# Attention with beacon keys and a gated feed-forward layer on one core: gate and value weights in two column blocks, under a newly searched instruction order

## The chip, the cores and the metric

The kernel runs on one core of a Trainium2 chip. The core has five engines with an instruction queue each: TensorE (PE in the profile, with PEld for its weight loads), VectorE (DVE), ScalarE (ACT), GpSimd (POOL) and SyncE (SP), and sixteen DMA engines that they share. The metric is device time in microseconds (us), the median of several executions.

## The reference

Inputs are q, k and v of shape 8 batches x 8 heads x 576 positions x 64, 16 extra "beacon" keys and values per head, and three weight matrices: gate and value of 512 x 1,536, output of 1,536 x 512. All are float32.

```
k_all = concat(beacon_k, k); v_all = concat(beacon_v, v)
scores = (q @ k_all.T) / 8, causal: the beacon keys are seen by every row
a = softmax(scores);  x = a @ v_all, heads side by side -> 4608 x 512
out = (relu(x @ w_gate) * (x @ w_val)) @ w_out      -> 4608 x 512, float32
```

## The kernel before

**Attention.** Each batch's q and k are loaded by SP's queue into staging tiles, rounded to bfloat16 (POOL or DVE), transposed on TensorE (L553, L626) and copied from PSUM (L493 on ACT, L495 on DVE). Scores (L824, in 64 x 64 parts of the array; L874 for the last 16 rows of a batch) go to PSUM. DVE adds the mask and takes the row minimum of the negated scores (L772), ACT takes the exponential and its sum (L779), DVE the reciprocal (L785), POOL normalises (L790). The weights are transposed, for batch 0 on TensorE (L900), later by DMA (pTb from pb, pTa from pa), and multiplied with v (L920, for the last rows L943) into the transposed activations xT.

**Feed-forward layer.** Ten spans of positions (240, 336, seven of 512, 448) each go through 12 blocks nf of 128 hidden columns: four gate matmuls (L981), relu on ACT (L992), four value matmuls (L986), the product on DVE (L997). Output products (L1012) follow per 128 positions in three parts of four nf, are copied out and stored.

**Weights.** They stay in SBUF as wg_r, wv_r and wo_r (bfloat16). The function `weight` (L505 to L512) issues one DMA on POOL's queue that reads float32 and writes bfloat16, for all four row blocks of 128 and w columns from n0:

```
x = add("POOL", W_ISSUE, lambda t: nc.gpsimd.dma_start(
    d[:, ko:ko + kos, n0:n0 + w], s[:, ko:ko + kos, n0:n0 + w]), (), (), work, 0.1, move=W_MOVE * kos * w / 512,
    after=W0 + W_STEP * len(weight_in) / KM)
for i in range(kos):
    for c in range(n0, n0 + w, 512):
        weight_in[kind, ko + i, c] = x
```

The loop at L1034 calls it for gate and value of each entry of W_COLS, then three times for the output weights (four blocks of 128 rows each). Below, v0 or g512 mean the transfer of value columns from 0 or gate columns from 512; wo0, wo4 and wo8 the three of the output weights. Blocks nf=0 to 3 use columns 0 to 511, nf=4 to 7 columns 512 to 1,023, nf=8 to 11 columns 1,024 to 1,535.

**The order.** Nothing is scheduled at run time. Work is entered in a plan as tasks with engines, costs and dependences; a search outside this file has put them into one list, and `replay` (L1067) issues the tasks as the string ORDER lists them: an entry is a task's number, a letter for the engine where there is a choice (a ACT, v DVE, g POOL) and the numbers of the buffers that it takes. f4:7 stands for four fill matmuls on ident (L1064) into PSUM bank 7, which do no work of the kernel; they stand in the first 32 us. Each engine works its own part of the list in order; semaphores hold an instruction until its inputs are there. So the order of one engine's queue is fixed, and an instruction that waits holds up all behind it on that engine.

POOL's order of transfers is v0, g0, v512, g512, wo0, v1024, g1024, then much later wo4 and wo8. HELD (L45) ties three loads of batch 1 to weights while an order is searched: at L563 a one-element memset of the staging tile on POOL stands ahead of such a load, and the load on SP's queue comes after the memset.

On TensorE, gate nf=0 of the first span is the 43rd task; gate nf=4, the first to use columns from 512, comes after the value product of batch 0's first head pair that uses L920 on pTb and the last 64 x 64 scores of batch 0's second group. After it come the scores of batch 0's last rows (L874), another value product and gate nf=5.

Of the kernel before, what the change touches and what calls it, by code (L numbers as in the profile page):

```python
# [54 lines left out]
W_COLS = [(0, 512), (512, 512), (1024, 512)]  # L55
# [22 lines left out]
10 1 22:0 2 26:1 34:3 0 4 30:2 23v:0.0 8 38:4 24:0 9 5 f4:7 42:5 27g:1.0 7 25v 48:7 28:1 46:6 35v:0 31v:2 36:3 29v 32:2 50:0 f3:7 37v 33a 54:1 f2:7  # L78
39v:1 410:4.5.0.0 58:2 11 431:6.0 6 40:1 411 43g:2 12 412 41a 423 44:2 413 45a 49g:0 422 3 436 414 448:3.1.0.0 62:7 415 421 f12:7 432 47g 426 68:5 450
416 459 70:6 449 425 460 51g:0 451 469:2.4 424 66:4 f1:7 417 437 461 14 52:5 427 433 55v:1 470 53a 418 56:6 434 f8:7 474 428 463 419 57v 471 429 462  # L80
420 59v:2 486:5.6.0.1 475 430 472 63v:0 454 473 438 487 64:2 453 435 60:7 464 69v 439 491 452 440:4 61a 72:0 476 495:3.1 13 73 441v:0 492 f3:7 455 465
496 488 444:0 467 f2:7 16 65v 504:4.5 497 77:1 489 500 442:2 445a:0 458 f3:7 505 457 f1:7 501 466 513:6.0 493 456 509 446:3 506 477 f1:7 f3:7 502 498
468 514 447a 443a 15 478:3 510 71v 482:4 518 522:1.2 515 19 511 524 479a:0 523:5.6 67g 516 519 483v:0 480:3 512 528 484:4 481a 18 525 548:7.3.2.3 485v
529 549 90:5 494 557:1.2 91 1734:4 553 17 550 1738:0 562 1735:0 566:5.6 507 503 1739:1 f2:7 558 563 1736:4 508 567 1742:7 559 490 1737:0 554 526 520
499 1740:4 571 1743:2 575:1.0 81:3 568 517 1741:1 82 1744:2 576 86:4 572 584:3.4 527 f1:7 580 1746:5 577 521 532:7 569 530 560 586 1747:1 531 536:1
533a:0 1748:5 1745:2 534:6 74:1.1 1749:3 537a 540:2 564 535v 587 78:2.1 95:0 544:5 542:1 541v:1 125:7 538:6 581 570 588 573 585:2.3 551 565 543a 555
539v 1750:0 561 545v 610:6.7.0 590 1751:1 552 546:4 589 578 611 591 1754:0 579 75:5 612 1752:1 1755:0 582 592 547v 76a 1756:3 574 613 1758:2 1757:5
593 594:4 1753:4 1759:0 596:5 556 595v:2 598:1 1762:0 583 614 79:7 597v 1760:4 1763:1 615 599a 602:2 1761:6 80a 606:5 87:1 616:1 604:4 617v:0 83:0
600:3 603v:3 92:2 101:3 84:6 601a 88:7 113:4 605v 607a 93:0 96:0 618:3 105:1 85a 89v 20 109:2 608:2 94a 99:6 97:5 126:1.0 609v 1766:1 98a 1764:4 619a
127:6 620:0.2.0.1 102:2 1765:7 128a 635:3.5 1770:7 1767:2 621 21 643 103:6 628 1768:4 622 1771:0 106:0 104a 1772:1 1769:8 624 1774:7 114:2 1773:9  # L90
1778:4 629 623 123:4 1776:1 1775:1 644 1779:2 1780:6 121:5 110:1 631 1792:4 1777:10 133:1 636 630 650:7.0 137:2 1781:11 1793:0 1787:2 637 129:0 645
646 659 107:6 652 639 111:4 1782:1 632 625 638 647 651 649 108a 112v 115:3 1788 633 653 640 116v 627 654 665:6.5 658 626 674:3.4 634 661 666 1794:7
642 660 670 1783 667 100:1 655 676 671 657 1784 119:6 124 677 700:0.6.2.3 1795:12 1785a:0 122 141:4 1796:5 701 679 117:3 668 656 708 715:7.1 702 678
648 1789 134:1 709 1797:1 704 669 717 145:1 1800:4 176:5 662 1790a:1 1798:3 716 664 723 703 1802:5 663 718 1799:13 641 1801:2 1804:2 724 1786 120 711
675:3.4 672 705 680 1803:14 149:6 1805:0 681 1806:0 726 683 682 1808:2 719 1807:15 673 690:3 1812:5 710 1809:1 712 130:0.0 730:6.0 684 725 1810:7 720
732 686 713 1814:1 738 1813:2 721 731 685 714 1816:5 1811:8 118 131:2 739 734 1818:4 687 1815:1 1817:1 689 745:3.7 733 1819:2 1820:1 688 741 735 746
754:5.6 132a 736 695:1 740 1822:4 750 722 1821:1 1824:0 757 142:0 747 1823:11 1828:1 151:7 707 751 756 755:3.4 138:2 1825:2 727 1832:2 742 748 758 737
763 1826:7 706 1829:0 752 749 1830:0 759 152 1827:4 728 691:1 760 764 693:7 762 692a 1831:5 765 761 780:5.6.1 694v 139:1 781 135:0 753 1833:1 770:2
143:3 766 1836:7 140v 146:1 136a 1834:2 782 729 1837:2 767 147:4 144a 1835:6 1838:0 769 783 148v 744 696:1 698:2 784 1839:10 790:5.6.0.1 785 805:4.7
1840:3 792 160:1 768 791 786:0 799 743 794 1841 177:2.1 775:3 798 697a 813 793 1842 150:0 787v:1 699a 814 801 153:0 788:2 807 800 178:1 1843a:2  # L100
820:0.5 789v 161:2 773:6 179a 828 815 806 771:2 1845:3 795 829 809 156:0 821 808 772v 1846 164:1 816 822 180:7 774v 831 835:2.4 1847 823 840 830 1791
824 817 1850:6 832 172:6 833 841 825 836 170:3 826 844:0.1 1848a:0 819 778:5 810 846 837 834 776:7 1851 811 777a 838 847 796 779a 157:1 154:2 849
845:4.5 184:0 165:0 848 1852 853 839 188:1 192:2 166:3 802 155v 1853a:1 804 162:0 1849 158:7 1855:1 854 812 174:5 850 167v 855 173 168:4 1857:6 163v
852 1856:2 159v 1859:2 827 856 797 857 1858:8 870:7.0.2.3 1860:1 851 885:4.3 1863:5 871 893 872 185:2 860:2 1867:2 886 874 878 842 894 843 1861:6 873
887 1864:2 858 896 1865:7 1862:9 803 1868:0 171 879 1871:5 895 859 888 875 1866:10 818 880 900:6.1 889 169 1869:2 865:1 909 881 175 901 1875:3 908
1872:1 189:0.1 1870:11 911 915:7.4 181:1 902 1873:2 910 890 916 904 892 903 182:1 876 1879:0 183v 193:1 1876:2 210:7 1874:4 917 861:6 863:3 196:2 897
882 862a 912 920 202:6 924:1.2 1880:0 200:1 925:6.7 927 921 1877:5 918 905 926 919 864a 226:0 1881:0 877 1878:13 928 933 914 950:3.4.0 929 868:5 206:5
906 1844 934 866:1 1883:2 930 224:4 867v 935 931 1882:14 1854 186:1 891 1884:1 190:6 187v 1887:0 203:0 191a 951 936 907 194:2 1885:6 932 195a 937 952
197:2 1888:2 940:2 1889:7 1886:15 953 899 869v 1895:1 938 954 1890:0 198:3 207:1 204:0 1891:4 199a 883 205v 884 959:6.5.7.2.0.1 1892:0 939 208:3 218:6
913 961 1893:4 898 209a 220:2 973 211:2 960 1899:0 965 1894:1 955 964 962 1897:3 974 956:0 1896:1 1900:2 963 1901:6 1898:2 967 230:5 941:0 975 943:4  # L110
978 922 976 923 1903:1 977 214:7 944a 1902:3 227:1.0 942a 945:3 1904 966 979 221:1 980 986:5.3.4.6 225 1908:7 987 988 1913:0 215:0 998 991 981 968 201
1909 997 990 989 219 222:4 1910 999 242:1 992 256:6 957:5 1001 212:2 1911a:0 1905 213v 231:2.0 958a 1912 1000 216:5 970 238:2 1002 1906v:2 1914 234:7
993 217v 223 1007:3.4.6.7 946:1 995 250:4 1015 948:2 972 1918:5 949a 971 1016 252:3 985 1009 1915 1017 1907 947v 982 284:5 1008 983 1018 1105:1.2.1
268:0 228:6 1916a:1 1919 1106 1010 1917 1019 235:0 1107 1920 1011 229v 969 246:7 1108 1003 239:1 1923:3 1921v:0 1004 1109 1032:4.0.7.1.2.3 1110 1924:0
1925:2 1034 994 1111:1 996 1931:5 1033 1046 1038 1926:4 251:0 232:6 1927:3 1047 1932:2 264:4 1037 1012 1048 1013 1050 1929:2 1036 1051 1021 236:4 1035
1928:1 1933:5 233v 243:2 1039 1049 1040 1014 272:1 244:7 240:3 1930:5 247:0 237a 1022:0 1935:6 1053 245v 253:1 1112:4 1052 241v 1020 1936:0 1939:0
1934:6 1005 248:2 1113v 257:2 1059:1.5.3.7 249a 254:6 1940:1 1061 1943:4 255a 1070 260:6 1060 1937:2 1041 1944:2 1071 1043 1062 1947:6 1074 984 1054
# [205 lines left out]
def kernel(  # L323
# [774 lines left out]
```

## Time and profile before

| | |
|---|---|
| median of 2 runs | 399.56 us (399.12 to 400.01) |
| the profiled execution | 399.52 us, of which its span, first to last instruction, 397.6 us |
| granted TensorE clock, mean | 0.999 |
| busy: PE, DVE, ACT, POOL | 96%, 69%, 68%, 58% of the span |
| moved by DMA | 68.89 MB, 173 GB/s on average |
| first matmul, first gate matmul (L981), first L1012 | 4.37, 27.55, 51.79 us |

Times in the views are microseconds from the first instruction. A view by stretch gives the busy time of each engine in it; a timeline gives start, length, engine, line, operation, tiles, count, and in brackets how long the engine stood idle before and what released it. Matmul lengths overlap (a matmul's record includes its latency), so start times tell more than lengths. A row "A <- B: total, times, longest" says how long A waited for B. Time to landing runs from a DMA's issue to its semaphore.

### The profile page before, as it was taken

The page shows a single profiled execution, that of the slowest core. Times are in us where ns is not written, and L with a number is a line of the kernel's source. Part 1 is how long each engine was busy: PE and PEld are TensorE (multiplying, and loading weights), DVE is VectorE, ACT ScalarE, POOL GpSimd, SP SyncE. Part 2 cuts the span into 40 slices and gives each one's busy share as a digit, 9 for nine tenths or more (in the row PEclk, how much of TensorE's full clock was granted, in tenths as well). Part 3 has the DMA queues.
Part 4 walks back from the last instruction along what each step waited for, and adds up shares of the span by engine and source line. Part 5 has one row for each costly group of instructions (what it writes and reads, how often), then busy time and mean ns, then how long its engine had stood idle before and what let it go on. Part 6 is the DMA issues. An engine that isn't in the chain of part 4 may idle for free.

```text
span 397.6 us, 10026 instructions
## 1 busy us (share of the span) xinstructions
PE 380.1 (96%) x3384; PEld 199.7 (50%) x3428; DVE 274.2 (69%) x1008; ACT 270.3 (68%) x842; POOL 231.0 (58%) x447
## 2 busy tenths in 40 slices
PE   5789999999999999999999899999999999999996
PEld 3557855655454455454444454445444445444453
DVE  5899799888976888877876778567946832331230
ACT  1899699897877687789777789688746731332322
POOL 3799779959785789268827787663853650000000
PEclk9999999999999999999999999999999999999999
DMA  7999999999999999968997999988897556001102
GB/s 183 218 181 237 193 230 235 195 230 236 215 234 205 313 177 203 181 186 177 202 205 215 197 202 198 209 162 167 169 180 161 101 105 168 28 0 54 54 26 94
DMA packets 184100, 68.89 MB, mean 173 GB/s; under 512 B 158384, under 2 KB 179504, under 8 KB 184048
## 3 DMA queue, kind: packets, MB, share of 16 engines
q1 hardware_dynamic: 179216, 63.46, 74.5%
q0 software_dynamic: 4752, 4.72, 7.3%
q8 instruction: 27, 0.44, 0.5%
q14 instruction: 25, 0.20, 0.1%
q10 hardware_dynamic: 80, 0.07, 0.1%
HBM read 38.54 MB, written 9.44 MB: 121 GB/s over the span
## 4 chain that ended last, share of the span: by engine, by line
PE 83%; DMA 3%; issue 1%; DVE 1%; POOL 0%; ACT 0%; DVEq 0%
PE f L1012 22%; PE f L986 22%; PE f L981 22%; PE f L824 6%; PE f L920 6%; PE f L553 2%; DMA pTb<-pb 2%; DMA pTa<-pa 2%; PE f L943 1%; PE f L626 1%; PE f L874 1%; DVE f L772 0%; PE f L900 0%; POOL pa L790 0%; DVE kT L495 0%
## 5 line engine op out<-in xcount | busy, mean ns | idle before, releaser
L790 POOL TENSOR_SCALAR pb<-pb,small 128x384 bf16<-128x384 bf16 (+8 forms) x272 | 142.1, 538 | 45.5 <-DVE small L785 43.9
L779 ACT ACTIVATE pb<-f,small 128x448 bf16<-128x448 f32 (+8 forms) x272 | 144.8, 551 | 24.5 <-DVE small L772 19.7
L772 DVE CUSTOM_DVE_ANT_0 f<-f,mask 128x64 f32<-128x64 f32 (+8 forms) x288 | 136.3, 507 | 20.1 <-PE f L824 11.0
L997 DVE TENSOR_TENSOR hT<-g,f 128x512 bf16<-128x512 f32 (+3 forms) x120 | 74.4, 629 | 55.3 <-PE f L986 30.2
L981 PE MATMUL f<-xT,wg_r 128*128 128x512 bf16 (+3 forms) x466 | 108.1, 357 | 0.9 <-issue 0.2
L986 PE MATMUL f<-xT,wv_r 128*128 128x512 bf16 (+3 forms) x465 | 106.8, 357 | 1.2 <-issue 0.3
L1012 PE MATMUL f<-wo_r,hT 128*128 128x512 bf16 (+3 forms) x441 | 100.3, 374 | 1.5 <-issue 1.0
L992 ACT ACTIVATE g<-f 128x512 f32<-128x512 f32 (+3 forms) x120 | 65.8, 563 | 49.3 <-PE f L981 31.0
L981 PEld LDWEIGHTS <-wg_r 128*128 128x128 bf16 x480 | 45.0, 98 | 45.2 <-issue 2.5
L986 PEld LDWEIGHTS <-wv_r 128*128 128x128 bf16 x480 | 44.5, 98 | 44.2 <-issue 3.0
L1012 PEld LDWEIGHTS <-hT 128*128 128x128 bf16 (+3 forms) x456 | 41.9, 100 | 47.0 <-issue 2.9
L779 ACT ACTIVATION_READ_ACCUMULATOR pb<-f,small 128x1 f32 x272 | 60.0, 221 | 0.0
L542 POOL TENSOR_SCALAR h<-st 128x512 bf16<-128x512 f32 (+1 forms) x87 | 46.8, 547 | 22.5 <-DMA st<-in_q_dram 5.0
L772 DVE DVE_READ_ACCUMULATOR2_ANT small<- 128x1 f32 x296 | 41.2, 139 | 0.1
L824 PE MATMUL f<-kT,qT 64*64 64x64 bf16 (+7 forms) x640 | 34.6, 296 | 1.6 <-ACT pb L779 0.7
L497 POOL TENSOR_SCALAR v<-st 128x512 bf16<-128x512 f32 (+1 forms) x38 | 23.3, 616 | 19.7 <-DMA st<-in_v_dram 19.6
L493 ACT CAST xT<-f 128x240 bf16<-128x240 f32 (+2 forms) x46 | 16.1, 376 | 22.6 <-PE f L920 22.5
L785 DVE RECIPROCAL small<-small 128x2 f32<-128x2 f32 (+3 forms) x136 | 19.7, 160 | 12.0 <-ACT pb L779 10.8
L920 PE MATMUL f<-pTb,v 128*64 128x320 bf16 (+3 forms) x488 | 27.0, 254 | 0.4 <-DMA pTb<-pb 0.4
L824 PEld LDWEIGHTS <-qT 64*64 64x64 bf16 x640 | 14.7, 107 | 22.6 <-issue 17.7
L920 PEld LDWEIGHTS <-v 128*64 128x64 bf16 (+1 forms) x512 | 21.0, 109 | 9.9 <-issue 5.1
L553 PE MATMUL f<-ident,h 128*128 128x128 bf16 (+1 forms) x224 | 19.8, 222 | 5.7 <-DVE h L542 5.0
(62 smaller groups left out, 216.1 us busy)
## 6 DMA issues: line engine op xcount, KB each, us to landing
out_dram<-osb SPq DMA_DIRECT2D x34, 256.0 KB, 2.7
st<-in_k_dram SPq DMA_DIRECT2D x28, 256.0 KB, 4.6
st<-in_q_dram SPq DMA_DIRECT2D x28, 256.0 KB, 4.0
st<-in_v_dram SPq DMA_DIRECT2D x24, 256.0 KB, 4.6
st<-in_q_dram SPq DMA_DIRECT2D x16, 128.0 KB, 3.8
st<-in_k_dram SPq DMA_DIRECT2D x16, 128.0 KB, 4.1
st<-in_v_dram SPq DMA_DIRECT2D x8, 224.0 KB, 4.5
wv_r<-in_moe_w_val_dram POOLq DMA_DIRECT2D x3, 512.0 KB, 9.2
```

The costliest lines, as they stand in the source:

```text
L542: (nc.gpsimd if x.engine == "POOL" else nc.vector).tensor_scalar(to, src, by, 1.0, ALU.mult, ALU.mult)
L553: nc.tensor.matmul(to, h16.tile[:rows, a * P:(a + 1) * P], ident[:rows, :rows], start=True, stop=True)
L772: nc.vector.tensor_tensor_reduce(out=view(i, n - m), in0=view(i, n - m), in1=msk, scale=1.0, scalar=at(7) if m < n else 3.0e38, op0=ALU.ad ...
L779: nc.scalar.activation(ph.tile.rearrange("p a n -> p (a n)")[:, a:a + n], view(i), AF.Exp, bias=at(i), scale=-1.0, accum_out=at(4 + i))
L790: nc.gpsimd.tensor_scalar(one, one, at(8 + i), 1.0, ALU.mult, ALU.mult)
L824: nc.tensor.matmul(banks[k][b_].tile[64 * i:64 * i + 64, off:off + n], t.q.tile[r, 2 * g + i, 64 * j:64 * j + 64], t.kT.tile[r, 2 * g + i, ...
L920: nc.tensor.matmul(ps.tile[64 * hh:64 * hh + 64, d0:d0 + w], t.v.tile[:rows, c, D * h:D * h + D], rhs(64 * hh), start=(c == 0), stop=(c == ...
L981: nc.tensor.matmul(psg.tile[:, :mt], wg_r[:, ki, nf * P:(nf + 1) * P], xT[:, ki, m0:m0 + mt], start=(ki == 0), stop=(ki == KM - 1))
L986: nc.tensor.matmul(psv.tile[:, :mt], wv_r[:, ki, nf * P:(nf + 1) * P], xT[:, ki, m0:m0 + mt], start=(ki == 0), stop=(ki == KM - 1))
L992: r = add("ACT", c_act(mt), lambda _, psg=psg, g=g: nc.scalar.activation(g.tile[:, :mt], psg.tile[:, :mt], AF.Relu), (a,), (psg, g), -1000 ...
L997: hid.append(add("DVE", c_dve(mt), lambda _, psv=psv, g=g, nf=nf: nc.vector.tensor_mul(hT[nf].tile[:, :mt], g.tile[:, :mt], psv.tile[:, :m ...
L1012: nc.tensor.matmul(ps[c].tile[64 * c:64 * c + rows, :w], hT[nf].tile[:, t0:t0 + rows], wo_r[:, nf, w * c:w * c + w], start=(nf == 0), stop ...
```

## The change

It has two parts, made together. W_COLS goes from three entries to two, so that the gate and value weights come in blocks of 512 and 1,024 columns, each in one transfer: four transfers for both matrices where six stood, seven with the output weights where nine stood. Two tasks fall away, so all later numbers are lower by two. And ORDER is another list, found by a longer search for the new tasks; 93 lines as before, nearly all of them different as text.

```
-W_COLS = [(0, 512), (512, 512), (1024, 512)]
+W_COLS = [(0, 512), (512, 1024)]
...
 ORDER = """
-10 1 22:0 2 26:1 34:3 0 4 30:2 23v:0.0 8 38:4 24:0 9 5 f4:7 42:5 27g:1.0 7 25v 48:7 28:1 46:6 35v:0 31v:2 36:3 29v 32:2 50:0 f3:7 37v 33a 54:1 f2:7
+11 4 20:0 3 2 24:1 32:3 0 5 1 28:2 f4:7 21v:0.0 9 36:4 8 12 22:0 40:5 25g:1.0 f2:7 46:7 26:1 33v:0 44:6 f2:7 6 27a 29v:2 f1:7 34:3 23v 30:2 48:0 f2:7
...
```

Read per engine, the new list does this:

- POOL issues v0, g0, v512 (columns 512 to 1,535), g512 (512 to 1,535), wo0, and later wo4 and wo8. The four that come first have the same places as before among POOL's normalisations (g512 one normalisation later); wo0 has moved behind a v copy and two memsets.
- The three memsets of held loads of batch 1 come sooner: the first right behind v0 instead of right ahead of g0 (nine normalisations lie between), the other two right ahead of wo0 instead of behind v1024 and some normalisations behind g1024.
- TensorE has the same tasks ahead of gate nf=4 as before, in nearly the same order, with 43 fill matmuls where 46 stood. Further on neighbours have changed places, seldom by more than a few tasks.
- The choice between ACT and DVE differs for 54 copies: 31 go from ACT to DVE and 23 the other way.
- The three parts of the last spans' output products are somewhat differently mixed with gates and values; the last task is the same 64-row output block.

More of the change, by code (lines that the diff above doesn't have):

```diff
@@ L82 @@
[L82 to L117, printed above, removed]
@@ new lines @@
+492 1738:4 573:1.0 1741:2 497 514 1739:1 561 1744:5 574 515 582:3.4 570 1742:2 567 510 528 518 578 575 530:7 519 558 1745:0 1743:2 534:1 531a:0 529
+584 1746:5 532:6 76:2.1 1747:3 535a 538:2 533v 585 542:5 568 540:1 539v:1 536:6 579 72:1.1 586 549 583:2.3 576 541a 537v 550 93:0 1748:0 543v 587
+123:7 608:6.7.0 588 1749:1 544:4 577 609 589 1752:0 559 107:2 553 1750:1 562 610 1753:0 545v 563 73:5 611 1754:3 590 571 1751:4 554 592:4 74a 612
+1760:0 591 580 1755:5 593a:2 594:5 581 596:1 1756:2 595v 572 1758:4 1757:0 77:7 597a 81:0 604:5 1759:6 600:2 1761:2 78a 85:1 99:3 602:4 601v:3 605a
@@ new lines @@
+1841a:2 771:6 819 814 769:2 820 1843:3 807 826 154:5 177v 821 1844 162:1 806 827 1789 770a 772v 822 1845 170:6 813 823 178:7 828 833:2.4 815 793
+842:0.1 1846a:0 795 834 1848:6 829 151:0 838 835 1847 774:7 808 830 776:5 845 809 775a 155:1 839 152:2 844 1849 163:0 172:5 777a 846 168:3 156:7 810
+843:4.5 166:4 847 831 164:3 852 816 160:0 157a 1853:1 186:1 824 836 848 840 153a 851 825 1850 794 161v 1854:2 849 165a 1857:2 850 854 837 853 1855:1
+817 858:3 1858:1 855 883:4.3.2.3 1856:8 169 1851a:0 868:7.0 1865:2 870 841 1861:5 187:0.1 869 884 872 892 856 1859:6 885 871 1866:0 179:1 800 891
@@ new lines @@
+1114 265a 1959:1 1040 1055 1127 1117 1075 1961:0 1029a 273 1098:3 1960:13 1131 1066 1115 1965:7 1130 1129 1118 275:1.1 1083 1116 1258:2.3.0 1962:2
+1963:5 1067 1128 1120 1259 1084 1966:0 276:1 1967:0 1964:14 1119 1085 1133 277v 1969:7 1093:0 1260 1968:15 1261 1974:4 1132 1262 1121 1139:5.3.1.2
+1263 1975 1141 1122 269 1150 1970 1140 283:1 1144 1142 1971 285:2.1 1143 1151 1264:0 1145 1976 1152 1154 1979:3 1972v:0 1153 278:3 1155 1977v:1
+1160:0.1.5.6 1134 1094:7 289:0 1162 1099:2 1096:4 1095a 1156 1973 1169 1159 1101:7 1161 316:2 1097a 1980 305:6 1100v 1164 298:7 1168 279:0 1265:4 1163
@@ new lines @@
+318:1 1146 1984:2 1125 1170 1165 1102v 1137 280:1 1266v 1171 1981 1158 281v 1166 1185:7.0.4.5.2.3 1982v:2 1147 1993:1 1123 1186 1983 1187 291:3 1167
+1989:3 1994:1 1172 1200 320:4 317:1 1190 1985 1173 1990:0 1199 1188 1191 1189 1991:6 1157 1148 1203 1202 1192 1986 1149 1204 1201 1992:0 1124 1193
+1997:7 1138 1175:3 1987v:0 1206 286:0.1 1194 1205 1212:3.2.4.6 1998:0 287v 292:1 1995:5 288a 1213 1214 2005:1 1207 1225 1216 1208 2001:0 1174 1217
+1996:1 296:2 1135 1228 290:0 1224 1999:7 299:2 1223 300:5 2003:5 1215 1136 1227 2000:2 2002:2 1198 2007:3 1180:1 1209 2004:12 2006:0 2009:7 1226
@@ new lines @@
+2182 1629 2185 1635 2177 2188:2 399 1636 1637 2189 1630 2186v:2 1632 404:6 1612 1564:1 393 1566:6 1622 1565v 1639 2190 1567a 1587 1601 402:0 2193:5
+2191v:0 1638 406:7 2195:7 2187 1631 2194:0 1614 2197:0 2196:4 1588 1723:4.5.1 2198:1 1650:2.6.3.7.2.3 1640:3 1724 2205:0 1725 1666 407 1726 2201:1
+1665 1603 1652 405 2199:4 2202:2 1667 1600 2206:0 2203:5 1654 1664 1645:1 2200:5 2209:1 1669 1651 1668 2204:15 2207:4 1670 1653 2211:3 1657 2208:3
+2210:2 2213:5 1658 2212:8 1671 1641:6 1677:3.0.1.4 1656 2217:7 2192 1655 1680 1642a 1659 2215:2 1679 1662 2218:0 1688 2214:2 1672 2219:6 1678 1676
@@ L171 @@
+2348:0 2353:4 2322a:1 2351:0 2354:0 2350:2 2355:2 2352:1 2361:5 2357:3 2362:2 2365:7 2358:1 2317a:2 2363:0 2318 2359:3 2323 2364:4 2369:4 2360:3
+2367:0 2356:2 2370:1 2366:0 2371:2 2373:1 2372:10 2375:4 2368:8 2374:2 2377:6 2376:11 2382:0 2378 2379 2383 2380a:0 2381 2384 2387:5 2385a:1 2388 2386
+2389 2392:4.6 2390v:2 2391 2395:1 2393v:0 2396 2394
 """
```

119 lines of the change are left out of this document (66 added, 53 removed), and 6 rows, old and new, of the table ORDER.

## Prediction

> **What bounds the kernel now.** I read the page first (busy shares and DMA queues), then busy time by stretch of the span, then who TensorE waited for, and last the early timeline of TensorE beside the weight transfers.
>
> ```profile
> span 397.6 us, 10026 instructions
> PE 380.1 (96%) x3384; PEld 199.7 (50%) x3428; DVE 274.2 (69%) x1008; ACT 270.3 (68%) x842; POOL 231.0 (58%) x447
> q1 hardware_dynamic: 179216, 63.46, 74.5%
> q0 software_dynamic: 4752, 4.72, 7.3%
> ```
>
> ```profile
> 0.00:10.00 10.00, 5.33 (x45) 3.00 (x45) 5.75 (x42) 1.79 (x4) 3.60 (x15) 1.00 0.75 183
> 10.00:20.00 10.00, 7.91 (x75) 5.27 (x76) 8.96 (x51) 8.65 (x39) 8.00 (x17) 1.00 1.06 218
> 20.00:30.00 10.00, 8.56 (x100) 5.53 (x98) 10.00 (x38) 10.00 (x34) 9.88 (x20) 1.00 1.17 181
> 30.00:40.00 10.00, 9.85 (x130) 7.67 (x129) 9.37 (x39) 9.64 (x29) 9.16 (x18) 1.00 1.19 238
> ...
> 80.00:320.00 240.00, 235.22 (x2197) 116.00 (x2231) 184.48 (x670) 186.49 (x590) 162.44 (x311) 1.00 0.93 195
> 320.00:380.00 60.00, 59.74 (x326) 28.80 (x330) 17.41 (x31) 16.55 (x32) 3.56 (x7) 1.00 0.26 69
> ```
>
> The columns of the second fence are stretch, length, busy time of PE, PEld, DVE, ACT and POOL, granted clock, DMA share, GB/s. Until 30 us the softmax engines set the pace (DVE and ACT full, POOL 9.88 of 10 us). From 30 us on TensorE is busy 98 to 99.6% in every stretch. So whatever TensorE loses after 30 us is lost for the whole kernel, unless one of its later waits gets shorter in return. Those waits are few; from 36 us to the end, all on data and above 0.1 us are these:
>
> ```profile
> PE f L943 <- DMA pTa<-pa: 1.4, 1, 1.4
> ...
> PE f L920 <- DMA pTb<-pb: 0.4, 1, 0.4
> ...
> PE f L1012 <- DVE kT L495: 0.2, 1, 0.2
> ```
>
> At most 2.0 us can therefore be given back. The profiled execution took 399.52 us around its span of 397.6, so 1.92 us lie outside; it stands 0.04 us below the median 399.56.
>
> **The change, wide transfers.** Gate and value columns 512 to 1,535 now come in one transfer each. The wait that matters is that of gate block nf=4 (columns 512 to 639): it waited for a 512-column transfer, the fourth issued on POOL's queue, and now waits for the fourth again, which is twice as wide and follows one twice as wide. Issue and landing of the transfers, in order of issue (g0, v512, g512 with wo0, v1024, g1024; the first, v0, was issued at 13.6):
>
> ```profile
> L507 POOL DMA_DIRECT2D wg_r<-in_moe_w_gate_dram x1: 788/788/788, 19.0 to 19.0; - x1
> DMA to landing us min/median/max: 7.1/7.1/7.1
> L507 POOL DMA_DIRECT2D wv_r<-in_moe_w_val_dram x1: 788/788/788, 20.1 to 20.1; - x1
> DMA to landing us min/median/max: 9.2/9.2/9.2
> L507 POOL DMA_DIRECT2D wg_r<-in_moe_w_gate_dram x1: 788/788/788, 23.1 to 23.1; - x1
> L507 POOL DMA_DIRECT2D wo_r<-in_moe_w_out_dram x1: 747/747/747, 23.9 to 23.9; - x1
> DMA to landing us min/median/max: 9.9/11.7/13.4
> L507 POOL DMA_DIRECT2D wv_r<-in_moe_w_val_dram x1: 788/788/788, 25.9 to 25.9; - x1
> DMA to landing us min/median/max: 15.7/15.7/15.7
> L507 POOL DMA_DIRECT2D wg_r<-in_moe_w_gate_dram x1: 788/788/788, 27.2 to 27.2; - x1
> DMA to landing us min/median/max: 17.7/17.7/17.7
> ```
>
> Issue plus landing gives g0 26.1, v512 29.3, g512 33.0 (23.1 + 9.9), wo0 37.3 (23.9 + 13.4), v1024 41.6, g1024 44.9. Issues are 0.8 to 3 us apart, landings 3.2 to 4.3: the queue works one transfer off after the other, and a transfer behind others waits for their bytes, not for its issue.
>
> After g0 the changed kernel moves v512 to 1,535 and g512 to 1,535 ahead of everything else: four 512-column blocks where two stood. Bounds for the landing of the second: if bytes alone count, it lands as the fourth block after g0 did, at 41.6. If a transfer had one price whatever its width, it would land as the second did, at 33.0. The nearest rows are the two queues of the page. q0: 7.3% of 16 x 397.6 us over 4,752 packets is 98 ns for 993 bytes written, 1,986 read (it casts float32 to bfloat16); q1: 74.5% over 179,216 is 26.4 ns for 354 bytes. A line through both over bytes read has 11 ns fixed and 0.044 ns a byte; a packet twice as long then takes 185 ns, 1.89 times as much. So four blocks, 15.5 us from 26.1 to 41.6, become 15.5 x 1.89 / 2 = 14.6, and the wide gate block lands at 40.7. I take that, as the load of those 15 us on the other queue is the same.
>
> ```profile
> 35.81 0.43 PE L824 MATMUL f<-kT,qT 64*64 64x512 bf16 x4
> 36.17 0.58 PE L981 MATMUL f<-xT,wg_r 128*128 128x240 bf16 x4
> 36.69 0.43 PE L874 MATMUL f<-kT,qT 128*32 128x512 bf16 x8
> 37.05 0.71 PE L920 MATMUL f<-pTb,v 128*64 128x320 bf16 x10
> ```
>
> Gate nf=4 is the row at 36.17. In the new order exactly the same TensorE instructions stand ahead of it, but for three fill matmuls (43 for 46), so it is reached at about 36.2 again. Its weight load then waits until 40.7: **4.5 us**, between 0 (33.0) and 5.4 (41.6). Behind it in TensorE's queue stand the last-row scores of batch 0 (L874), its value products (L920) and the remaining gates and values, and behind those ACT's relu, DVE's products and batch 1's scores; TensorE is full afterwards, so all 4.5 us stay.
>
> By the Trainium skill, "DMA: Bandwidth & Descriptors", Anatomy of one DMA — SWDGE (gpsimd) path, a transfer costs about 2.0 us plus its bytes at 436 GB/s, which speaks for wide ones. By that rule 1 MB read takes 4.4 us (the trace's steps are 3.2 to 4.3, so the trace hides part of the fixed share) and 2 MB 6.8; two wide ones would land at 39.7, and the sum would be 1 us lower.
>
> **Two issues less.** Each occupies POOL 0.79 us (788 ns above); v1024 and g1024 at 25.9 and 27.2 fall away, 1.6 us in a stretch where POOL is full. Normalisations come sooner, but TensorE then only reaches gate nf=4 sooner and waits longer: nothing. Without that wait it could bring up to 1.6 us.
>
> **Other weights.** Columns 1,024 on landed at 44.9 and land at 40.7, ahead of their use: no gain, since TensorE did not wait there. wo0 is now issued behind both wide blocks and lands near 40.7 + 4.3 = 45.0; its first product stood at 51.8 (row below) and moves later with the rest: nothing, and 4 us more delay would still be covered.
>
> ```profile
> 51.79 1.07 PE L1012 MATMUL f<-wo_r,hT 128*112 128x512 bf16 x4
> ```
>
> **Held loads of batch 1.** Three one-element memsets on POOL move ahead (one before g0's issue, two before wo0's), so SP starts batch 1's loads some us sooner, with the queues behind them unchanged. They take DMA time from the wide transfers in the same 15 us, already in the 41.6; nothing extra.
>
> **The searched order.** Beyond the start it is the old order with neighbours swapped: counted in TensorE instructions at their durations in this profile, the work between a head's scores and its value products differs by at most about 1 us everywhere. Three terms are visible. After the first gate TensorE changes between array shapes 154 times instead of 158; the load wait at such a change is this row's 17.7 / 48 = 0.37 us at most, of which part is overlapped, and nothing at least: 4 x 0.15 = **-0.6**, between 0 and -1.5.
>
> ```profile
> PEld L824 <- issue: 17.7, 48, 0.6
> 221.83 0.67 PE L943 MATMUL f<-pTa,v 128*128 128x32 bf16 x20 [1.40 <-DMA pTa<-pa]
> ```
>
> One more four-matmul group (0.86 us) stands ahead of batch 5's last-row product, whose wait was 1.40: **-0.7**, between 0 and -0.9. Copies swap between ACT and DVE, net eight to DVE, about 0.5 us each; both are idle 30% of the span: nothing, and 4 us on DVE if that cover were gone.
>
> Sum: 4.5 - 0.6 - 0.7 = +3.2; span 400.8, time 400.8 + 1.9 = **402.7 us**.
>
> **Rivals.** *No stall.* If a wide transfer takes at most 1.4 times a narrow one (two steps of 5.05 us from 26.1 to 36.2), gate nf=4 finds its weights, and the small gains are left: 399.5 - 1.3 = 398.2, down to 396.6 with POOL's 1.6. For it speaks that bigger transfers can only be more efficient; against it that q0 packets cost nearly by their bytes. The sign turns at a landing of 37.5. Chance 0.18.
>
> *The clock falls as well.* An idle TensorE loses its clock:
>
> ```profile
> 392.00:394.00 2.00, 1.87 (x27) 1.23 (x24) 0.04 (x1) 0.60 (x2) 0.00 (x0) 1.00 0.10 33
> 397.00:397.60 0.60, 0.00 (x0) 0.00 (x0) 0.00 (x0) 0.00 (x0) 0.00 (x0) 0.56 0.00 0
> 12.06 2.74 PE L1064 MATMUL f<-mask,ident 128*128 128x256 bf16 x12
> 15.54 0.71 PE L1064 MATMUL f<-mask,ident 128*128 128x256 bf16 x5
> ```
>
> The last matmul ends at 394.0, and a mean of 0.56 over the last 0.6 us means half speed from 397.07: 3.1 us of idleness. A cold start shows how long it lasts: twelve fills at 12.06 run at about 0.21 us each for 2.7 us, those at 15.54 at 0.11. Half speed for 2.7 us costs 1.4 us: 404.1. Against it: 3.1 us is seen once, and 4.5 is little more. The Trainium skill, "TensorE: Matmul & The Clock Gate", Part 1, says the gate watches a free-running window of about 3.4 us and closes after a wholly idle one; the trace's 3.1 is near it, and 4.5 us would contain such a window in a third of the phases. Chance 0.22.
>
> *New waits later.* The order may miss on other transfers as it does here: if TensorE's 2.0 us of data waits after 36 us double, 404.7. Against it: the distances hardly changed. Chance 0.08.
>
> **How the numbers follow.** Forecast 0.45, without the clock's fall; no stall 0.18, clock 0.22, later waits 0.08, anything else 0.07. Range 398.5 to 405.3: it leaves out the better part of the no-stall case (0.1) and half of the rest (0.08), and takes in 41.6 with a cold clock (405.0). The forecast's own range is 400.5 to 403.7. About 2% (8 us, 391.6 or 407.6) is what a measurement of this kernel tells from no change; no case reaches either end, so within 2% has 0.93, faster 0.02, slower 0.05 (two mishaps together).
>
> **What would show it.** In the changed profile the fourth weight transfer lands near 40.7, the first gate matmul of columns 512 on has 3 to 5 us of idle before it put down to the weight transfer, TensorE's slice there is below 8 tenths, and every later landmark (first L1012, last score, last matmul) is later by about that much less 1.3. The clock digit there tells the second rival. Wrong would be: a landing by 36, TensorE at gate nf=4 much later than 36, or a delay that shrinks over the following 280 us.

## The result and the profile after

| | before | changed |
|---|---|---|
| median of 2 runs | 399.56 us (399.12 to 400.01) | 404.56 us (402.97 to 406.15) |
| ratio of the changed to the kernel before | | 1.0107 [1.0066, 1.0148] |
| the profiled execution, its span | 399.52, 397.6 us | 402.97, 401.3 us |

The changed kernel is 1.1% slower, inside the 2% taken as no difference, and near the forecast of 402.7 us. A ratio is worked out over the executions, with its 95% interval in brackets, and is not exactly the quotient of the two medians. The page of its profiled execution: TensorE has 4.7 us more busy time on record, and POOL's queue (q0) moves the same bytes in 3,696 packets where 4,752 stood.

```profile
span 401.3 us, 10054 instructions
PE 384.8 (96%) x3425; PEld 200.6 (50%) x3425; DVE 280.9 (70%) x1013; ACT 270.1 (67%) x837; POOL 230.1 (57%) x445
q1 hardware_dynamic: 179216, 63.46, 73.5%
q0 software_dynamic: 3696, 4.72, 6.9%
```

The weight transfers from g0 on, in order of issue (instruction length, start, and below it the time to landing):

```profile
L507 POOL DMA_DIRECT2D wg_r<-in_moe_w_gate_dram x1: 788/788/788, 19.1 to 19.1; - x1
DMA to landing us min/median/max: 6.9/6.9/6.9
L507 POOL DMA_DIRECT2D wv_r<-in_moe_w_val_dram x1: 788/788/788, 20.4 to 20.4; - x1
DMA to landing us min/median/max: 11.1/11.1/11.1
L507 POOL DMA_DIRECT2D wg_r<-in_moe_w_gate_dram x1: 788/788/788, 24.1 to 24.1; - x1
DMA to landing us min/median/max: 14.0/14.0/14.0
```

So g0 lands at 26.0, the wide value block at 31.5 and the wide gate block at 38.1 (24.1 + 14.0). TensorE's early timeline shows who waits for that; in the second row 1.18 us of idle time stand before the first matmuls that use columns from 512 (gate nf=4):

```profile
36.51 0.43 PE L824 MATMUL f<-kT,qT 64*64 64x512 bf16 x4
38.12 0.58 PE L981 MATMUL f<-xT,wg_r 128*128 128x240 bf16 x4 [1.18 <-DMA wg_r<-in_moe_w_gate_dram]
38.63 0.44 PE L874 MATMUL f<-kT,qT 128*32 128x512 bf16 x8
```

Busy time by stretch (stretch, length, PE, PEld, DVE, ACT, POOL, clock, DMA share, GB/s):

```profile
20.00:30.00 10.00, 7.94 (x96) 4.99 (x95) 10.00 (x39) 9.53 (x30) 7.26 (x16) 1.00 1.16 201
30.00:40.00 10.00, 8.71 (x110) 6.29 (x108) 8.67 (x35) 8.61 (x25) 9.14 (x17) 1.00 1.14 240
80.00:320.00 240.00, 236.51 (x2243) 116.01 (x2241) 188.49 (x669) 182.25 (x576) 161.63 (x308) 1.00 0.95 199
320.00:380.00 60.00, 60.00 (x336) 28.66 (x331) 19.20 (x41) 17.18 (x37) 6.67 (x13) 1.00 0.24 57
```

From 30 to 40 us TensorE's busy time falls from 9.85 to 8.71. In the ten microseconds before that it falls too, from 8.56 to 7.94: the new order's start is slower as well. What TensorE waited for on data from 36 us to the end:

```profile
PE f L553 <- POOL h L542: 2.3, 2, 1.5
PE f L981 <- DMA wg_r<-in_moe_w_gate_dram: 1.2, 1, 1.2
PE f L920 <- DMA pTb<-pb: 1.1, 1, 1.1
PE f L1012 <- DMA wo_r<-in_moe_w_out_dram: 0.2, 1, 0.2
```

Where 2.0 us stood before, 4.8 stand now, and the longest item is new: two transposes (L553) that wait for POOL's rounding of a loaded q or k tile (L542). In the timeline those and the value products' wait stand here:

```profile
93.59 0.62 PE L553 MATMUL f<-ident,h 128*128 128x128 bf16 x8 [0.78 <-POOL h L542]
...
111.90 0.88 PE L920 MATMUL f<-pTb,v 128*64 128x320 bf16 x16 [1.08 <-DMA pTb<-pb]
...
119.59 0.40 PE L553 MATMUL f<-ident,h 128*128 128x128 bf16 x4 [1.49 <-POOL h L542]
```

How late a kernel is against the kernel before, read at the start of the first last-row scores (L874) of a batch, in us:

| batch | 0 | 1 | 2 | 3 | 4 | 5 | 6 | 7 |
|---|---|---|---|---|---|---|---|---|
| start in the kernel before | 36.69 | 74.50 | 107.65 | 132.72 | 160.82 | 206.50 | 255.13 | 300.82 |
| changed kernel, later by | 1.95 | 1.93 | 2.73 | 4.11 | 4.93 | 5.13 | 3.66 | 3.63 |

The last matmul starts 3.6 us later (397.2 for 393.6). By the rows this is 0.7 at the start (L824 at 36.51 for 35.81), 1.2 for the weights, 0.8 and 1.5 for the two L553 waits, 1.1 - 0.4 for pTb and 0.2 for the output weights, less the 1.4 of the pTa wait, which is gone: 3.7. The sum agrees; batch by batch it does not quite (0.8 us appear between batches 3 and 4 without a data wait of that size). Nor is one execution the kernel: the kernel before took from 398.85 to 402.33 us in the 24 executions of the first set of experiments, so a difference of a microsecond between two profiles can be chance. The two parts of the change had to be taken apart.

### The profile page after: what moved, and what is told of

Its sections match the earlier page's. It is cut to its first block, busy times and chain, and to the rows that moved or that the text cites. A ratio compares the mean times of both kernels' runs of the same rounds, so it can differ in the third digit from the quotient of the medians.

```text
span 401.3 us, 10054 instructions
## 1 busy us (share of the span) xinstructions
PE 384.8 (96%) x3425; PEld 200.6 (50%) x3425; DVE 280.9 (70%) x1013; ACT 270.1 (67%) x837; POOL 230.1 (57%) x445
## 3 DMA queue, kind: packets, MB, share of 16 engines
q0 software_dynamic: 3696, 4.72, 6.9%
## 4 chain that ended last, share of the span: by engine, by line
PE 83%; DMA 9%; DVE 2%; POOL 2%; ACT 1%; SPq 1%; issue 1%; POOLq 0%; DVEq 0%
PE f L1012 23%; PE f L981 22%; PE f L986 21%; PE f L920 6%; PE f L824 6%; DMA wg_r<-in_moe_w_gate_dram 3%; DMA wo_r<-in_moe_w_out_dram 2%; PE f L553 2%; DMA st<-in_k_dram 2%; DMA st<-in_q_dram 1%; PE f L943 1%; ACT pb L779 1%; PE f L626 1%; SPq L677 1%; DMA st<-in_beacon_k_dram 1%; PE f L900 1%
## 5 line engine op out<-in xcount | busy, mean ns | idle before, releaser
L790 POOL TENSOR_SCALAR pb<-pb,small 128x512 bf16<-128x512 bf16 (+8 forms) x272 | 143.1, 547 | 65.9 <-DVE small L785 52.2
L772 DVE CUSTOM_DVE_ANT_0 f<-f,mask 128x192 f32<-128x192 f32 (+8 forms) x288 | 136.7, 507 | 21.5 <-PE f L824 11.9
L981 PE MATMUL f<-xT,wg_r 128*128 128x512 bf16 (+3 forms) x480 | 108.7, 358 | 1.2 <-DMA wg_r<-in_moe_w_gate_dram 1.2
L1012 PE MATMUL f<-wo_r,hT 128*128 128x512 bf16 (+3 forms) x456 | 102.7, 374 | 0.3 <-DMA wo_r<-in_moe_w_out_dram 0.2
L992 ACT ACTIVATE g<-f 128x512 f32<-128x512 f32 (+3 forms) x120 | 65.4, 562 | 54.9 <-PE f L981 38.6
L981 PEld LDWEIGHTS <-wg_r 128*128 128x128 bf16 x480 | 44.5, 98 | 46.5 <-issue 3.5
L542 POOL TENSOR_SCALAR h<-st 128x512 bf16<-128x512 f32 (+1 forms) x87 | 47.3, 554 | 24.2 <-DMA st<-in_q_dram 7.7
L779 ACT ACTIVATION_READ_ACCUMULATOR pb<-f,small 128x1 f32 x272 | 58.8, 216 | 0.0
L772 DVE DVE_READ_ACCUMULATOR2_ANT small<- 128x1 f32 x296 | 41.5, 140 | 0.1
L824 PE MATMUL f<-kT,qT 64*64 64x64 bf16 (+7 forms) x640 | 34.4, 297 | 2.0 <-DVE xT L495 0.9
L920 PE MATMUL f<-pTb,v 128*64 128x320 bf16 (+3 forms) x488 | 27.0, 253 | 1.1 <-DMA pTb<-pb 1.1
L920 PEld LDWEIGHTS <-v 128*64 128x64 bf16 (+1 forms) x512 | 21.1, 109 | 10.9 <-issue 5.7
L824 PEld LDWEIGHTS <-qT 64*64 64x64 bf16 x640 | 14.6, 107 | 22.2 <-issue 16.8
L553 PE MATMUL f<-ident,h 128*128 128x128 bf16 (+1 forms) x224 | 21.1, 228 | 4.5 <-POOL h L542 3.3
L493 ACT CAST xT<-f 128x320 bf16<-128x320 f32 (+2 forms) x39 | 14.9, 390 | 15.3 <-PE f L920 15.0
```

Of the source, the lines that this page charges most:

```text
L542: (nc.gpsimd if x.engine == "POOL" else nc.vector).tensor_scalar(to, src, by, 1.0, ALU.mult, ALU.mult)
L553: nc.tensor.matmul(to, h16.tile[:rows, a * P:(a + 1) * P], ident[:rows, :rows], start=True, stop=True)
L772: nc.vector.tensor_tensor_reduce(out=view(i, n - m), in0=view(i, n - m), in1=msk, scale=1.0, scalar=at(7) if m < n else 3.0e38, op0=ALU.ad ...
L779: nc.scalar.activation(ph.tile.rearrange("p a n -> p (a n)")[:, a:a + n], view(i), AF.Exp, bias=at(i), scale=-1.0, accum_out=at(4 + i))
L790: nc.gpsimd.tensor_scalar(one, one, at(8 + i), 1.0, ALU.mult, ALU.mult)
L824: nc.tensor.matmul(banks[k][b_].tile[64 * i:64 * i + 64, off:off + n], t.q.tile[r, 2 * g + i, 64 * j:64 * j + 64], t.kT.tile[r, 2 * g + i, ...
```

## The experiments

Two theories stood against each other. A: the lost time is gate nf=4's wait for the wide block, and the new order is harmless. B: much of it is the new order, through waits that have nothing to do with the width. A third question came up with the first experiment: what the idle time does to the clock. Each ratio is to the kernel before on the same chip. Fill matmuls, where added, do no work of the kernel.

**The changed kernel again**, no edit.

> The changed kernel once more, in more rounds, to learn its time and its spread. Both theories: 402.5 to 405.5, gate nf=4 waits about 1.2 us for its weights. If the waits of TensorE for POOL's rounding (L553) and for a transposed block (L920) near 93 to 118 us come back in this profile, they belong to the order; if they are gone or elsewhere, they are chance of one execution.

Measured: 408.21 us, 1.0175 [1.0143, 1.0207], more than the first time. The wide gate block was issued at 23.8 and took 16.1 us, landing at 39.9 instead of 38.1. TensorE's timeline:

```profile
36.27 0.43 PE L824 MATMUL f<-kT,qT 64*64 64x512 bf16 x4
39.98 0.98 PE L981 MATMUL f<-xT,wg_r 128*128 128x240 bf16 x4 [3.27 <-DMA wg_r<-in_moe_w_gate_dram]
```

The wait is 3.27 us, and the same four gate matmuls take 0.98 us where they took 0.58. The busy times by stretch of 2 us tell why; the clock is the third number from the end:

```profile
36.00:38.00 2.00, 0.71 (x12) 0.29 (x8) 1.78 (x8) 1.29 (x3) 2.00 (x5) 1.00 1.14 243
38.00:40.00 2.00, 0.02 (x1) 0.02 (x2) 0.00 (x0) 0.00 (x0) 0.90 (x2) 0.83 1.20 236
40.00:42.00 2.00, 2.00 (x16) 0.90 (x18) 0.37 (x1) 0.94 (x3) 0.00 (x0) 0.50 1.18 251
42.00:44.00 2.00, 2.00 (x15) 1.39 (x12) 1.38 (x8) 0.41 (x3) 1.45 (x3) 0.50 0.32 80
44.00:46.00 2.00, 2.00 (x18) 1.72 (x16) 1.03 (x4) 1.23 (x5) 1.16 (x3) 0.50 0.01 2
46.00:48.00 2.00, 2.00 (x28) 1.94 (x26) 0.69 (x1) 1.30 (x4) 2.00 (x4) 0.96 0.04 8
```

TensorE counts as busy through the slow stretch; only the clock and the number of matmuls in two microseconds (15 to 18 instead of 28) show the loss. A mean of 0.83 means half speed from 39.3 (0.34 of 2 us lost at half rate is 0.68 us), and 0.96 means full speed again from 46.2. The lag is +4.2 us at batch 0's last rows and +6.5 at batch 1's, where the first profile had 1.95 and 1.93: the cold stretch cost 2.3 us beside the wait. It was not this execution alone: the mean clock of all five was 0.979 to 0.992. The L553 waits (2.7 us in two) and the pTb wait (0.8 us) came back as well. So the changed kernel has no single time: its weights land about where the clock's limit lies. A third measurement, in the next set:

> The changed kernel once more, beside the runs sent with it. Both theories: 404 to 408, with gate nf=4 waiting 1 to 3.5 us.

Measured: 404.29 us, 1.0123 [1.0083, 1.0162]; the block landed at 37.7, the wait was 1.12 us, the clock stayed at 1.00 in the profile, and an L553 wait was there again (1.5 us). In four of the six executions the mean clock was 0.992 to 0.996.

**The old order with the wide blocks.** The ORDER of the kernel before, without the entries of v1024 and g1024 and with all higher task numbers two lower:

```
-W_COLS = [(0, 512), (512, 512), (1024, 512)]
+W_COLS = [(0, 512), (512, 1024)]
```

> The old order with the wide transfers alone: v1024 and g1024 taken out of the list, v512 and g512 1,024 columns wide. Transfer theory (the late wide gate block is the loss, directly or by what it sets off later): 403 to 405. Order theory (the transfer costs only its wait, the rest is the new order): gate nf=4 waits 36.2 to about 38.1, so 401 to 401.6, and no new waits behind it.

Measured: 402.66 us, 1.0059 [1.0036, 1.0082].

```profile
35.94 0.43 PE L824 MATMUL f<-kT,qT 64*64 64x512 bf16 x4
38.86 0.58 PE L981 MATMUL f<-xT,wg_r 128*128 128x240 bf16 x4 [2.49 <-DMA wg_r<-in_moe_w_gate_dram]
```

The start is the old one (35.94 beside 35.81), the wait is 2.49 us, the clock holds, and no L553 wait appears. The lag is 2.7 us at batch 0, 3.4 at batch 2 and 2.15 at batch 7. The width by itself costs 0.6%, and the profile shows the loss mainly at this one place. But the profiled execution, 401.48 us, is the shortest of twelve: in ten of the others the mean clock was 0.994 to 0.996, so the median contains a loss of clock that this trace does not show.

**The new order with the narrow blocks.** The changed kernel's ORDER with task numbers for nine transfers; v1024 and g1024 (18, 17) put back right behind wo0 (19):

```
-W_COLS = [(0, 512), (512, 1024)]
+W_COLS = [(0, 512), (512, 512), (1024, 512)]
...
-... 17 1732:4 ...
+... 19 18 17 1734:4 ...
```

> The new order with 512-column transfers alone: v1024 and g1024 put back right behind wo0. Transfer theory: the loss is gone, 399 to 400. Order theory: only the wait of 1.2 us is gone, 402 to 403.5, with the waits near 93 to 118 us still there.

Measured: 401.77 us, 1.0027 [1.0004, 1.0051]. Gate nf=4 finds its weights (g512 landed at 32.2, its use is at 36.96). What is left of the change costs about 1.1 us by the ratio, between what the two theories gave, and its interval barely leaves out no cost at all. The L553 and pTb waits between 92 and 122 us are there too (3.7 and 1.0 us), but the profiled execution is the longest of the twelve (405.38 us), so their lengths say little.

**The new order with the narrow blocks in the place of the wide ones**, v1024 right behind v512 and g1024 right behind g512, so that the same bytes stand ahead of wo0 as in the changed kernel. The edit to the kernel of the last experiment:

```
-... 445a:0 16 f3:7 ... 524 15 510 ... 81:3 19 18 17 1734:4 ...
+... 445a:0 16 18 f3:7 ... 524 15 17 510 ... 81:3 19 1734:4 ...
```

> The new order with 512-column transfers in the order in which the wide ones moved their bytes: v512, v1024, g512, g1024, then wo0. Gate nf=4 then needs the third block behind g0, not the fourth. If the wait is only a matter of bytes ahead of the block, it lands near 36 and the time is that of the new order with narrow transfers, +0.1 to +0.6% on the kernel before; if narrow transfers are slower per byte by as much as the first traces suggest (3.9 against 3.0 us a block), it lands near 37.5 and waits about 1 us, +0.4 to +0.8%.

Measured: 402.77 us, 1.0069 [1.0038, 1.0100]. The block of gate nf=4 landed at 35.0 (24.6 + 10.4), nearer to the 36 of bytes alone than to 37.5. The gate ran without a wait, though the start was the slowest of all:

```profile
37.06 0.43 PE L824 MATMUL f<-kT,qT 64*64 64x512 bf16 x4
37.43 0.58 PE L981 MATMUL f<-xT,wg_r 128*128 128x240 bf16 x4
```

Its waits from 36 us on are the changed kernel's without the one for the gate block:

```profile
PE f L920 <- DMA pTb<-pb: 1.5, 1, 1.5
PE f L553 <- POOL h L542: 1.1, 1, 1.1
...
PE f L1012 <- DMA wo_r<-in_moe_w_out_dram: 1.0, 1, 1.0
```

So theory B has its part: with no width at all, the new order costs 0.3 to 0.7%. The lag is 1.3 us at batch 0, 3.5 at batch 3 and 3.0 at batch 7. The landings also weigh the width: from g0 (25.7) to g1024 (38.6) the four narrow blocks took 12.9 us, the two wide ones in three profiles of the changed kernel 12.0, 12.7 and 12.0.

**Gate ahead of value, in the new order.** In the changed kernel the two wide issues exchanged (15 is the gate block, 16 the value block):

```
-... 443a:0 16 f3:7 ... 522 15 508 ...
+... 443a:0 15 f3:7 ... 522 16 508 ...
```

> The changed kernel with the two wide transfers exchanged, so that the wide gate block is issued and lands first (near 31.5) and the value block, needed 3 to 4 us later, near 38. Transfer theory: 399 to 400. Order theory: the wait of 1.2 us goes, 402 to 403.5.

Measured: 404.22 us, 1.0088 [1.0058, 1.0118]. The wide gate block landed at 32.3, ahead of its use at 36.78; the wide value block at 39.0, just as its first use came up (39.02). The wait is gone and most of the loss is not: L553 waits of 1.4 us together and a pTb wait of 1.2 stand in this profile too. Nor is this loss the order's alone: in four of the seven executions the mean clock was 0.995 or 0.996, and the profiled one (402.17 us, clock 0.998) does not show where they lost it.

**Gate ahead of value, in the old order**: the same exchange in the kernel with the old order and wide blocks.

> The old order with wide transfers, the gate block ahead of the value block. If the wide transfers cost only through gate nf=4's wait: value nf=4, needed near 38.3, waits at most 1 us, and the time is that of the kernel before, -0.3 to +0.3%. If wide transfers also cost elsewhere: +0.5 to +0.9%, as the new order with the gate first.

Measured: 400.03 us, 1.0000 [0.9975, 1.0026].

```profile
36.16 0.58 PE L981 MATMUL f<-xT,wg_r 128*128 128x240 bf16 x4
...
38.44 0.99 PE L986 MATMUL f<-xT,wv_r 128*128 128x240 bf16 x8
```

Gate nf=4 is back at 36.16 to within 0.01 us, the first values of the wide block (landed at 38.4) follow at 38.44, and the span is 397.2 beside 397.6. This settles what width costs in the old order: the seven transfers, two of them wide, cost nothing within a quarter of a per cent if the one that is used first is issued first. The two issues that POOL saves are worth nothing that can be seen.

**Fills in the wait**, in the changed kernel: sixteen fill matmuls right ahead of gate nf=4 (task 1748).

```
-... 93:0 1748:0 543v ...
+... 93:0 f16:7 1748:0 543v ...
```

> The changed kernel with sixteen fill matmuls (about 1.8 us, no part of the result) ahead of gate nf=4, where TensorE otherwise stands idle for its weights. Clock theory (most of the loss beyond the wait itself is the half-speed clock after an idle stretch of over 3 us): the clock stays full, 2 to 4 us faster than the changed kernel beside it. Rival (the wait alone counts): no faster, up to 0.6 us slower where the wait is shorter than the fills.

Measured: 403.03 us, 1.0087 [1.0053, 1.0121], beside 1.0123 [1.0083, 1.0162] for the changed kernel on the same chip; the intervals overlap.

```profile
36.50 1.92 PE L1064 MATMUL f<-mask,ident 128*128 128x256 bf16 x16
38.26 0.57 PE L981 MATMUL f<-xT,wg_r 128*128 128x240 bf16 x4
```

The block lands at 37.7 while the fills still run, and the gate runs behind them, about half a microsecond after the landing. Neither kernel lost its clock in its profile here. Over all executions the mean clock was 0.992 to 0.996 in four of six without the fills and 0.996 in one of seven with them, so the fills seem to have kept it; what that is worth the overlapping intervals leave open. A longer wait can tell more.

**A long wait, with and without fills.** In the old order with wide blocks, the wide gate block (15) and wo0 (17) exchanged, so that the gate block lands later still; in the second kernel forty fills besides, ahead of gate nf=4.

```
-... 445a 441a 15 476:3 ... 520:1.2 513 17 509 ...
+... 445a 441a 17 476:3 ... 520:1.2 513 15 509 ...
...
-... 553 537v 1748:0 559 ...
+... 553 537v f40:7 1748:0 559 ...
```

> The old order with wide transfers and wo0 issued ahead of the wide gate block, so that gate nf=4 waits about 3.4 us longer than with the wide transfers alone (landing near 42.2, wait near 5.9 us). If a wait of this length costs only itself: about 5.9 us over the kernel before, +1.5%. Clock theory: the clock falls during the wait in nearly every execution, half speed for 3 to 7 us after it, so 1.5 to 3.5 us more: +1.9 to +2.4%.

> The same with forty fill matmuls (about 4.3 us, no part of the result) ahead of gate nf=4, so that TensorE idles under 2 us and its clock stays. Clock theory: 1.5 to 3.5 us faster than the long wait without fills, about +1.5% on the kernel before. Rival (only the wait counts): the same as without fills.

Measured without fills: 408.41 us, 1.0204 [1.0165, 1.0244]. Its gate row and its clock:

```profile
42.93 0.98 PE L981 MATMUL f<-xT,wg_r 128*128 128x240 bf16 x4 [6.77 <-DMA wg_r<-in_moe_w_gate_dram]
```

```profile
38.00:40.00 2.00, 0.00 (x0) 0.00 (x0) 0.00 (x0) 0.00 (x0) 1.31 (x3) 0.70 1.10 234
40.00:42.00 2.00, 0.00 (x0) 0.00 (x0) 0.00 (x0) 0.00 (x0) 0.00 (x0) 0.50 1.11 285
...
46.00:48.00 2.00, 2.00 (x14) 1.61 (x13) 0.26 (x1) 1.37 (x5) 1.88 (x3) 0.50 0.02 4
48.00:50.00 2.00, 2.00 (x24) 1.71 (x23) 1.02 (x4) 0.50 (x3) 0.00 (x0) 0.74 0.03 8
```

Measured with fills: 406.88 us, 1.0160 [1.0124, 1.0197].

```profile
35.37 4.54 PE L1064 MATMUL f<-mask,ident 128*128 128x256 bf16 x40
...
42.48 0.58 PE L981 MATMUL f<-xT,wg_r 128*128 128x240 bf16 x4 [2.58 <-DMA wg_r<-in_moe_w_gate_dram]
```

Both reach gate nf=4 within 0.5 us of each other (42.93 and 42.48). With fills its four matmuls take 0.58 us, the clock stays at 1.00, and the lag is the same at batch 0 and batch 1 (6.3 and 6.2 us). Without, 0.98 us, and the lag grows from 7.2 to 10.3, of which 0.9 is an L553 wait: some 2.3 us for the cold stretch, as in the changed kernel's second profile. The medians differ by 1.5 us, with overlapping intervals, and the profiled executions are not typical: without fills it is the longest of its six (411.11 us), with fills the second shortest (405.48 us). The clock is the clearer evidence. Without fills its mean was 0.986 to 0.992 in all six executions, with them 0.996 to 1.000, so in some of these a shorter cold stretch may be left.

**Where the new order loses**, tried on the narrow kernel with the same bytes ahead of wo0: if POOL's roundings are late because the q and k loads were moved back on SP, earlier loads must remove the L553 wait. First three loads of batch 3 moved ahead, then thirteen of batches 2 to 4 put about where the old order has them:

```
-... 878 184:0 875 1862:9 ... 1878:13 196:2 919 ... 866:1 202:6 930 ...
+... 1857:1 184:0 860:3 ... 895 196:2 865:1 ... 908 202:6 1875:3 ...
```

> The new order with narrow transfers in the wide ones' byte order, and three loads of batch 3 moved ahead on SP's queue: one ahead of a transposition, one ahead of the next, one directly behind that. Load theory (TensorE's waits for POOL's rounding come from loads that the new order puts behind transpositions and later loads): the L553 wait near 118 us goes, about 1 us faster than the same kernel without the moves, +0.3 to +0.5%. Rival (these waits are covered by the next one, for a transposed block): no difference, +0.7%.

> The same, with all thirteen q and k loads of batches 2 to 4 that the new order has two or more places later on SP's queue than the old one moved to about their old place, as far as their staging tiles are free. Load theory: both L553 waits go, +0.1 to +0.4% on the kernel before, what is left being the later first gate matmul. Rival: +0.6 to +0.8% as without the moves.

Measured: 402.63 us, 1.0051 [1.0021, 1.0082], and 402.96 us, 1.0070 [1.0040, 1.0101], beside 1.0069 [1.0038, 1.0100] without the move. The wait near 118 us, at which the first move was aimed, stands neither in its profile nor in that of the kernel without the move. The wait near 94 us stands in both (1.3 and 1.1 us), so this pair of traces does not test the move. The second has these waits from 36 us on, the L553 wait now at 92 us:

```profile
PE f L553 <- POOL h L542: 1.3, 1, 1.3
PE f L920 <- DMA pTb<-pb: 1.1, 2, 0.7
PE f L1012 <- DMA wo_r<-in_moe_w_out_dram: 0.4, 1, 0.4
```

Waits stay, and the time does not change beyond the intervals. The places of the loads on SP are not the cause, or not alone; this theory is not borne out.

## Why the prediction was right, and where it was not

**The total was right by two errors of opposite sign.** The sum had +4.5 for the stall and -1.3 for the order. In the profile that came first the weights' wait is +1.2, and by its rows the remaining 2.4 of the 3.6 us are the order's. That the two errors nearly cancelled was luck: by the ratio of the second measurement the kernel would take 406.6 us (1.0175 x 399.56), above the prediction's range. Of the signs that it named, 3 to 5 us of idle before gate nf=4 came only in that second profile; the first had 1.18, and its slice from 30 to 40 us stayed at 8.7 tenths. The later landmarks did not gain 1.3 us on the wait but lost about 2 more.

**The stall: right in place and kind, too large in size.** Gate nf=4 is the one that waits, for the weight transfer, because a wide block lies ahead of its own. In its profile the old order with wide blocks shows the wait and little else, and gate ahead of value takes wait and loss away. The failing term is the landing at 40.7: it was 38.1, 39.9 and 37.7, so the wait was 1.2, 3.3 and 1.1 us instead of 4.5. The price of a packet was about right. From the page's q0 rows, 0.069 x 401.3 x 16 = 443 us of engine time, less 2,640 narrow packets at 97.7 ns, leaves 175 ns for each of the 1,056 wide ones (186 and 169 by the other two profiles; the prediction had 185). What was wrong was to carry the 15.5 us of four blocks over from the old profile: the narrow blocks, too, take 12.9 us when gate and value follow each other without wo0 between them. In the new order with narrow blocks and wo0 in its old place the four took 14.0 us (25.9 to 39.9), in its longest execution. Why that stretch was slower before was not tried. By the Trainium skill, "DMA: Bandwidth & Descriptors", Anatomy of one DMA — SWDGE (gpsimd) path, the prediction had worked out an estimate of 39.7, which lies inside the measured landings, at their late end; its 13.6 us for the two blocks is longer than the 12.0 to 12.7 measured.

**When gate nf=4 is reached: "at about 36.2 again" failed by some tenths.** Its predecessor L824 starts at 36.51, 36.27 and 36.16 in the changed kernel's three profiles and at 37.06 in the last narrow one, against 35.81 before and 35.94 and 35.80 in the two kernels with the old order and wide blocks. The same tasks ahead of it do not make the same start. In a view of the waits between 15 and 36 us the changed kernel has one that the kernel before lacks:

```profile
PE f L824 <- DVE xT L495: 0.9, 1, 0.9
```

So TensorE waited there for a copy by DVE; counting TensorE's tasks alone could not see it.

**The searched order: the sign was wrong.** -0.6 - 0.7 was forecast, +1.1 to +2.8 us was measured (0.27% and 0.69%, in two forms without a wide wait). The single terms: the pTa wait of 1.4 us did go, as forecast (-0.7 had been taken, -1.4 came). The array shapes gave nothing: idle weight-load time ahead of L824 fell from 17.7 to 16.8 us, but that ahead of L981 rose from 2.5 to 3.5 and ahead of L920 from 5.1 to 5.7. And new waits came: on POOL's rounding, on pTb, on the output weights. The step that failed is the argument that "the distances hardly changed": it compared only TensorE's work between a head's scores and its products, not the distance from a load over POOL's rounding to the transposes. Under the heading of new waits later this had been a rival with a chance of 0.08; it happened, in every profile of the changed kernel, along with the stall. In the first of them POOL itself stood idle ahead of late roundings, waiting for the loaded tiles:

```profile
116.56 0.62 POOL L542 TENSOR_SCALAR h<-st 128x512 bf16<-128x512 f32 x1 [3.52 <-DMA st<-in_q_dram]
118.91 1.20 POOL L542 TENSOR_SCALAR h<-st 128x512 bf16<-128x512 f32 x2 [1.73 <-DMA st<-in_k_dram]
```

So there the loads were late, not POOL. Why they are late in the new order stays open: moving thirteen of them on SP's queue did not change the time, and undoing the reordering of the start alone was not tried. Nor are such waits the new order's alone: one of 0.9 us stands in the old order with the long wait.

**The clock: a rival that came true in part of the executions.** It was given 0.22 and 404.1 us, and in the second measurement's profile the clock did fall, as the mean clock shows for all five of its executions and four of the third measurement's six. Two of its numbers were off: the cold stretch after the wait lasts 6.2 us, not 2.7, and costs 2.3 us, not 1.4. Between the first two profiles of the changed kernel, 402.97 and 407.56 us, the wait grew by 2.1 us and the cold stretch came to 2.3: together 4.4 of the 4.6 us between them.

**Neutral terms.** wo0 had cover to spare, as said: its first use, at 53.45 in the changed kernel, does not wait (it landed at 41.5, 25.5 + 16.0). The third output transfer, wo8, was not in the prediction's account. In the profile of the changed kernel's third measurement it lands at 59.0 (49.1 + 9.9), where its first user has come to wait for it:

```profile
L507 POOL DMA_DIRECT2D wo_r<-in_moe_w_out_dram x1: 791/791/791, 49.1 to 49.1; - x1
DMA to landing us min/median/max: 9.9/9.9/9.9
```

```profile
59.03 1.02 PE L1012 MATMUL f<-wo_r,hT 128*128 128x512 bf16 x4 [0.90 <-DMA wo_r<-in_moe_w_out_dram]
```

In the kernel before it was issued at 47.1 and landed at 56.5 (47.1 + 9.4). Two issues less brought nothing, as forecast; the kernel with the old order and gate ahead of value shows that directly.

No version was faster than the kernel before.

## What to carry to other kernels

When transfers are merged, the first use of any part waits for the last byte of the whole; so issue the merged transfers in the order of first use, and check the landing of the second one against its use. A wait of 3 us on an otherwise full TensorE costs more than itself (here 3.27 us of wait and 2.3 us of cold clock), since the clock falls and comes back late. A searched order has to be judged on its own, against the old one with the same transfers: here it hid a loss as large as the one that the diff suggests.

## What the runs showed of the hardware

- The clock fell after about 2.6 us of an idle TensorE (work ended at 36.7, half speed from 39.3; with the long wait at 36.2 and, by the mean of 0.70, from 38.8), where 3.1 us had been seen at the end of the kernel before. It stayed at half for 6.1 to 6.2 us after work began again (39.98 to 46.2, and 42.93 to 49.0 by the mean of 0.74). Forty fills in 4.5 us, followed by 2.58 us of idle, kept it at 1.00. The Trainium skill, "TensorE: Matmul & The Clock Gate", Part 1, has a free-running window of about 3.4 us of idleness for the fall and one of about 3.4 us of sustained work for the return. That return agrees with a window that was missed and one that counted; the fall after 2.6 us is sooner than a wholly idle window allows. From fall to return it was 6.9 and 10.2 us (39.3 to 46.2, 38.8 to 49.0), about two and three such windows.
- A packet of the casting queue twice as long took 175 ns instead of 98 (169 to 186 over three profiles): merging saved 5 to 14% of the engines' time per byte, and at most 0.9 us until the last of four blocks landed.
- The same kernel's wide gate block took 14.0, 16.1 and 14.0 us from issue to landing in three profiles.
